# Moving three kv products behind the q projection, and a carry product over all 128 rows, in a fused linear-attention and convolution kernel

## The chip, the cores and the metric

The kernel runs on one core of a Trainium2 chip. The metric is the device time of one execution in microseconds (us), the median of the runs shown.

## What is computed

x is 2048 by 448 (S by D). Two branches read it, and a gate per row mixes them. The reference, cut to what matters:

```python
g = sigmoid((x * gate_w).sum(-1, keepdims=True))
# branch a: linear attention, 16 heads of 28, not causal
q, k, v = split(x @ wqkv)
phi = lambda t: where(t > 0, t + 1, exp(t)) + 1e-6
kv = einsum("bhsd,bhse->bhde", phi(k), v)
z = einsum("bhsd->bhd", phi(k))
o = einsum("bhqd,bhde->bhqe", phi(q), kv) / (einsum("bhqd,bhd->bhq", phi(q), z)[..., None] + 1e-6)
a = o @ wo
# branch b: a long convolution with a kernel K made from A, C, dt, by FFT, plus a skip term
b = irfft(rfft(x) * rfft(K)) + x * D_skip
return g * a + (1 - g) * b
```

For the inputs in use K is flat to the precision needed, so branch b becomes a running sum over the rows, scaled per column, plus the skip; a slower general path follows under a flag and does not run.

## The kernel before

The 2048 rows are 16 chunks of 128 (`NC`, `P`). Each matrix product is split into a high and a low part in the format fp32r, and products are summed as high by high, low by high, high by low. The order of instructions is the order in which the code is written (`manual_schedule`): each engine works through its own queue in that order, and semaphores hold it where data is missing. PE is TensorE (matmuls; PEld its weight loads), ACT ScalarE, DVE VectorE, POOL GpSimd, SP the queue that issues the DMAs.

The main loop runs over `c` from 2 to 13. In one turn PE computes, in this order:

- k of chunk c+1: `project(c + 1, wkh, wkl, ...)`, eleven matmuls (L325). It reads `xt[c+1]`, the turned chunk, whose high half ACT casts and whose low half POOL subtracts (`split_t`, L234 and L230), one turn ahead.
- v products (`do_v`, L401, L402), which are the running sum inside a chunk by a triangle `tri`, from c = 5 on.
- the kv products g of chunk c, `do_g(c)`, eleven matmuls (L394) that add `xn[c]` (the plain chunk, split by `split_n`: ACT L240, POOL L230) against `pkh[c]` and `pkl[c]` to four PSUM banks. They are read after the last chunk alone.
- q of chunk c: `project(c, wqh, wql, D + 2, "q")`, eleven matmuls (L325) to the one PSUM bank with the tag q.

For c below 5, `do_g(c)` stands ahead of q; for c above 4 it stands behind q and what follows q.

ACT and DVE turn k into its feature: `k_feature` (ACT e L351, L352; DVE L353), `k_high` (ACT pkh L357), `k_low` (DVE pkl and the column sums zb, L363). `q_post` does it for q: ACT e (L371, L340), DVE t (L341) and pq (L344). In the turns c = 2 and 3 ACT and DVE also do half of the reductions over the 256 states that decide and scale K (`steps`: ACT L283, L284; DVE L285). At c = 3 DVE casts `tri` and `gcr` (L501, L502). At c = 4 small operations on four columns follow (`sm`, L273, L274, L292 to L302), and at c = 5 PE transposes their result (p, L306), between q and g of chunk 5.

`skip(c)` (POOL L246) multiplies a plain chunk by D_skip.

The carry of the running sum from chunk to chunk is made behind the loop. The last rows of the chunks' v sums are gathered by DMA in `u`, at rows 0 to 15 and 32 to 47 (`UL` = 32); ACT casts `u` to `uw`, POOL makes rows 32 on the low part, and one product z (L688) with the table `gcr` gives what enters each chunk. Then PE forms kv (L719) from the copies `gs` of g, DVE masks it (L725 to L732), ACT casts `kvh` (L736), DVE makes `kvl` (L739), and PE multiplies it with wo (m, L699). The last loop then turns pq (tr, L595) and multiplies (a, L620), and the outputs are written.

Of the kernel before, what the change touches and what calls it, by code (L numbers as in the profile page):

```python
# [42 lines left out]
GIN = 9 + NC  # L43
L1, L0 = 32, 64
UL = 32
UZ = 2 * UL
PAD = S + P
MAGIC = 1.5 * 2.0 ** 23
TWO_PI = 6.283185307179586
# [85 lines left out]
def gated_mix_kernel(ctx: ExitStack, tc: tile.TileContext, xin, wq_d, wvo_d, abc_d, ldt_d, dsk_d,  # L135
                     turn_d, cst_d, first_d, gin_d, lag_d, out):
    nc = tc.nc
    PE, ACT, DVE, POOL, SP = nc.tensor, nc.scalar, nc.vector, nc.gpsimd, nc.sync
# [21 lines left out]
    cst = const.tile([P, DJ + RX + 1], F32, name="cst")  # L160
    mask, gcat, sel = cst[:DJ, :DJ], cst[:UZ, DJ:DJ + RX], cst[:, DJ + RX:]
    gcr = const.tile([UZ, RX], F32R, name="gcr")
    ones = const.tile([P, P], F32R, name="ones")
    rows = const.tile([P, S], F32, name="rows")
    near, dsk = (rows[:, i * D:(i + 1) * D] for i in range(2))
    u = const.tile([UZ, D], F32, name="u")
    zb = const.tile([P, D], F32, name="zb")
# [23 lines left out]
    def load_x(c):  # L191
        r = xp.tile([P, XC], F32, name="xr", tag="xr")
        turned[c], plain[c] = r[:, :NAT], r[:, NAT:]
        SP.dma_start(out=r, in_=xin[c])
# [34 lines left out]
    def low(eng, o, r, h):  # L229
        eng.tensor_tensor(out=o, in0=r, in1=h.bitcast(F32), op=ALU.subtract)  # L230

    def split_t(c):
        w = xt[c] = xt_p.tile([P, 2 * NAT], F32R, name="xt", tag="t")
        ACT.copy(w[:, :NAT], turned[c])  # L234
        low(POOL, w[:, NAT:], turned[c], w[:, :NAT])

    def split_n(c):
        r, w = plain[c], xn_p.tile([P, NX], F32R, name="xn", tag="n")
        xn[c] = w
        ACT.copy(w[:, :XC - NAT], r)  # L240
        low(POOL, w[:, XC - NAT:], r[:, :D], w[:, :D])
        if c > 2:
            skip(c)

    def skip(c):
        POOL.tensor_tensor(out=y[:, c], in0=plain[c][:, :D], in1=dsk, op=ALU.mult)  # L246
# [82 lines left out]
    def project(*args, **kw):  # L329
        o, run = pieces(*args, **kw)  # L330
        run(11)
        return o
# [15 lines left out]
    def k_feature(c, o):  # L348
        e = tp.tile([P, D], F32, name="e", tag="e")
        pks[c] = o[:, :D]  # L350
        ACT.activation(e, pks[c], AF.Relu, scale=-1.0)  # L351
        ACT.activation(e, e, AF.Exp, scale=-1.0)  # L352
        DVE.scalar_tensor_tensor(out=pks[c], in0=pks[c], scalar=1.0, in1=e, op0=ALU.add, op1=ALU.max)  # L353

    def k_high(c):
        pkh[c] = tp.tile([P, 512], F32R, name="pkh", tag="pkh")[:, EDGE:EDGE + D]
        ACT.add(pkh[c], pks[c], 1e-6)  # L357

    def k_low(c):
        pk = pks.pop(c)  # L360
        pkl[c] = tp.tile([P, 512], F32R, name="pkl", tag="pkl")[:, EDGE:EDGE + D]
        for o, a, op in ((pkl[c], pkh[c].bitcast(F32), ALU.subtract), (zb, zb, ALU.add))[::-1 if c == NC - 1 else 1]:
            DVE.scalar_tensor_tensor(out=o, in0=pk, scalar=1e-6, in1=a, op0=ALU.add, op1=op)  # L363
# [6 lines left out]
    def q_post(c, o, mid=None):  # L370
        ACT.activation(e1[:, c:c + 1], o[:, D:D + 1], AF.Exp, scale=-1.0)  # L371
        feature(pq[:, c], o, mid)
# [13 lines left out]
    def do_g(c, blocks=range(4)):  # L386
        w = xn[c]
        for i in blocks:
            a = w[:, 64 + i * P:64 + (i + 1) * P]
            b = w[:, XC - NAT + 64 + i * P:][:, :P] if i < 3 else None  # L390
            seq = [(a, pkh[c]), (a, pkl[c]), (b, pkh[c])] if i < 3 else \
                  [(a, pkh[c]), (a[:, :64], pkl[c])][::1 if c == 0 else -1]
            for n, (a, b) in enumerate(seq):
                PE.matmul(g[i][:a.shape[1], :D], lhsT=a, rhs=b, start=c == 0 and n == 0,  # L394
                          stop=c == NC - 1 and n == len(seq) - 1)
# [3 lines left out]
    def do_v(c):  # L399
        v = vt[c] = ps.tile([P, 512], F32, name="v", tag="v%d" % (c % 2))  # L400
        PE.matmul(v[:, :D], lhsT=tri, rhs=xn[c][:, :D], start=True, stop=False)  # L401
        PE.matmul(v[:, :D], lhsT=tri, rhs=xn[c][:, XC - NAT:], start=False, stop=True)  # L402

    def v_post(c):
        t = tp.tile([P, D], F32, name="t", tag="v0")
        DVE.tensor_tensor(out=t, in0=vt.pop(c)[:, :D], in1=near, op=ALU.mult)  # L406
        if c < NC - 1:
            for k in (c, UL + c):
                SP.dma_start(out=u[k:k + 1], in_=t[P - 1:P])
            v_add(c, t)  # L410
        return t
# [5 lines left out]
    def steps(n):  # L417
        for _ in range(n):
            next(prep, None)
# [44 lines left out]
    for c in range(2, NC - 2):  # L464
        if c + 3 < NC:
            load_x(c + 3)
        if c == 2:
            SP.dma_start(out=cst, in_=cst_d)
        if c == 4:
            SP.dma_start(out=wvo, in_=wvo_d)  # L470
        vs = VS.get(c, ())
        ko = project(c + 1, wkh, wkl, D, "v1" if c in (2, 4) else "k")
        for v in vs[:1]:
            do_v(v)
        split_t(c + 2)
        k_feature(c + 1, ko)
        k_high(c + 1)
        if c > 5:
            for v in vs[:1]:
                v_post(v)  # L480
        k_low(c + 1)
        if c < 5:
            do_g(c)
        qo = project(c, wqh, wql, D + 2, "q")
        if c == 5:
            steps(1)
        else:
            for v in vs[1:]:
                do_v(v)
        q_post(c, qo)  # L490
        if c == 10:
            split_n(c + 2)
        if c == 5:
            v_post(0)
        else:
            for v in vs[1:]:
                v_post(v)
        if c < 5:
            steps(2 if c == 4 else 1)
        if c == 3:  # L500
            DVE.tensor_copy(tri, trir)  # L501
            DVE.tensor_copy(gcr, gcat)  # L502
        if c == 7:
            SP.dma_start(out=okr[:, None, :DJ], in_=oks[:, None, :])
        if c == 9:
            DVE.tensor_reduce(out=okr[:, DJ:], in_=okr[:, :DJ], op=ALU.add, axis=AX.X)
            DVE.tensor_copy(okn, okr[:, DJ:])
        if c > 4:
            do_g(c)
        if c == 5:  # L510
            do_v(1)
        if c < 4:
            skip(c - 1)
        if c != 10:
            split_n(c + 2)
        if c == 5:
            v_post(1)
        for j in {11: (0, 1), 12: (2, 3)}.get(c, ()):
            w = xn_p.tile([P, NX], F32R, name="wo", tag="n")[:DJ, :2 * D].rearrange("p (i d) -> p i d", i=2)
            woh.append(w[:, 0])  # L520
            wol.append(w[:, 1])
            ACT.copy(woh[j], wo[:, j])
            low(POOL, wol[j], wo[:, j], woh[j])
# [109 lines left out]
    c = NC - 2  # L633
# [3 lines left out]
    do_v(c + 1)  # L637
    uw = xt_p.tile([P, 2 * NAT], F32R, name="uw", tag="t")[:UZ, :D]
    k_feature(c + 1, ko)
    ACT.copy(uw, u)  # L640
    low(POOL, uw[UL:], u[UL:], uw[UL:])
    k_high(c + 1)
    k_low(c + 1)
    zh = tp.tile([P, D], F32R, name="zh", tag="w")
# [283 lines left out]
```

## Time and profile before

| | |
|---|---|
| median of 3 runs | 176.55 us (176.33 to 176.62) |
| the profiled execution | 176.31 us |
| its span, first to last instruction | 174.5 us |
| PE, PEld busy | 96%, 87% of the span |
| DVE, ACT, POOL busy | 65%, 55%, 69% |
| granted TensorE clock | 1.0 throughout |

The profile shows one execution. A row of a timeline gives start and length in us, engine, line of the code, operation, output<-input by the program's names, their shapes, how many instructions were merged into the row, and in brackets how long the engine sat idle before it and who ended that. Matmuls overlap, so a row of one matmul is longer (0.36) than the distance to the next (0.20). The tile names merge: k written to the bank v1 is called v.

### The profile page before, as it was taken

Reading aid. Unit: us, or ns where it says so; the run is one execution under the profiler, and the core shown is the slowest. Engines: PE = TensorE matmul, PEld = TensorE weight load, DVE = VectorE, ACT = ScalarE, POOL = GpSimd, SP = SyncE. Lnnn points to the kernel's source line nnn. Section 1 sums busy time; section 2 is a strip of 40 time slices with the busy share of each in tenths; the row PEclk is TensorE's granted clock in tenths of the full one; section 3 lists DMA queues with packets and bytes.
Section 4 is the critical chain, followed back from the end, with each engine's and each line's share of the span. In section 5 each row is a group of like instructions: output and inputs, shape, how many; then the busy total and the mean of one; then the engine's idle time right before and its main releaser. Section 6 shows DMA issues by size and latency. Waiting matters only on the chain.

```text
span 174.5 us, 2800 instructions
## 1 busy us (share of the span) xinstructions
PE 168.2 (96%) x876; PEld 151.5 (87%) x876; DVE 113.8 (65%) x240; ACT 96.5 (55%) x221; POOL 119.9 (69%) x128
## 2 busy tenths in 40 slices
PE   6999999999989999999999999999999999999991
PEld 2699999978789999999999999998999999999991
DVE  1747636498984663937537255487898998997551
ACT  3789395896454372534627366256475564664441
POOL 5167466557809996796996999529968998983100
PEclk9999999999999999999999999999999999999999
DMA  5999954087001230330404300000031221222212
GB/s 165 418 316 317 273 163 146 0 327 334 2 4 35 89 123 1 125 120 2 121 4 129 116 1 0 0 0 2 7 66 53 106 94 69 81 99 84 111 71 93
DMA packets 7963, 18.61 MB, mean 107 GB/s; under 512 B 2045, under 2 KB 4810, under 8 KB 7818
## 3 DMA queue, kind: packets, MB, share of 16 engines
q1 hardware_dynamic: 7946, 18.41, 31.2%
q8 instruction: 7, 0.11, 0.2%
q14 instruction: 10, 0.08, 0.2%
HBM read 14.38 MB, written 3.67 MB: 103 GB/s over the span
## 4 chain that ended last, share of the span: by engine, by line
PE 81%; DVE 8%; ACT 4%; POOL 3%; issue 2%; DVEq 0%; ACTq 0%; POOLq 0%
PE a L620 20%; PE g L394 16%; PE q L325 14%; PE k L325 13%; PE tr L595 4%; PE v L325 3%; PE q L252 2%; POOL y L246 2%; PE v L402 2%; PE v L401 2%; PE m L699 1%; DVE sm L274 1%; PE k L719 1%; PE tr L719 1%; ACT y L283 1%
## 5 line engine op out<-in xcount | busy, mean ns | idle before, releaser
L620 PE MATMUL a<-wk,th 128*128 128x448 f32 (+1 forms) x170 | 36.2, 359 | 0.0
L394 PE MATMUL g<-pkh,xn 128*128 128x448 f32 x112 | 35.5, 363 | 0.0
L620 PEld LDWEIGHTS a<-wk,th 128*128 128x128 f32 x170 | 29.5, 189 | 1.6
L325 PE MATMUL k<-wk,xt 128*128 128x448 f32 x132 | 29.4, 366 | 0.0
L325 PE MATMUL q<-wqh,xt 128*128 128x450 f32 x120 | 27.5, 366 | 0.0
L353 DVE SCALAR_TENSOR_TENSOR k<-k,e 128x448 f32<-128x448 f32 x12 | 7.6, 632 | 30.5 <-ACT e L352 30.5
L325 PEld LDWEIGHTS k<-wk,xt 128*128 128x128 f32 x132 | 24.5, 188 | 2.9 <-ACT wk L423 0.5
L230 POOL TENSOR_TENSOR xn<-xr,xn 128x448 fp32r<-128x448 f32 x16 | 18.8, 1178 | 11.6 <-ACT xn L240 11.2
L414 POOL TENSOR_TENSOR y<-y,t 128x448 f32<-128x448 f32 x16 | 18.7, 1169 | 11.4 <-DVE t L406 11.4
L325 PEld LDWEIGHTS q<-wqh,xt 128*128 128x128 f32 x120 | 22.5, 189 | 1.8
L394 PE MATMUL g<-pkl,xn 128*128 128x448 f32 x64 | 23.3, 364 | 0.0
L394 PEld LDWEIGHTS g<-pkh,xn 128*128 128x128 f32 x112 | 21.0, 188 | 2.2
L533 POOL TENSOR_TENSOR prod<-pq,zb 128x448 f32<-128x448 f32 x16 | 18.4, 1154 | 4.3 <-ACT zb L656 3.0
L351 ACT ACTIVATE e<-k 128x448 f32<-128x448 f32 x12 | 6.5, 545 | 25.5 <-PE k L325 25.4
L246 POOL TENSOR_TENSOR y<-xr,rows 128x448 f32<-128x448 f32 x16 | 18.5, 1155 | 0.0
L230 POOL TENSOR_TENSOR xt<-xr,xt 128x512 fp32r<-128x512 f32 x14 | 18.1, 1295 | 0.4 <-ACT xt L234 0.4
L558 POOL TENSOR_TENSOR pn<-pq,den 128x336 f32<-128x336 f32 x16 | 12.1, 754 | 5.9 <-ACT den L547 4.1
L625 DVE SCALAR_TENSOR_TENSOR ot<-y,og,a 128x448 f32<-128x448 f32 (+1 forms) x17 | 10.7, 629 | 5.0 <-PE a L620 5.0
L603 DVE TENSOR_TENSOR th<-tr,th 128x512 fp32r<-128x512 f32 x16 | 11.0, 690 | 2.5 <-ACT th L602 2.0
L357 ACT ACTIVATE pkh<-k 128x448 fp32r<-128x448 f32 x12 | 6.6, 546 | 10.0 <-DVE k L353 10.0
L394 PEld LDWEIGHTS g<-pkl,xn 128*128 128x128 f32 x64 | 11.2, 174 | 0.9
L602 ACT CAST th<-tr 128x512 fp32r<-128x512 f32 x16 | 9.4, 590 | 4.5 <-PE tr L595 4.2
(151 smaller groups left out, 307.1 us busy)
## 6 DMA issues: line engine op xcount, KB each, us to landing
xr<-in SPq DMA_DIRECT2D x15, 512.0 KB, 5.9
out<-ot SPq DMA_DIRECT2D x15, 224.0 KB, 1.9
pq<-in SPq DMA_DIRECT2D x4, 448.0 KB
wvo<-in SPq DMA_DIRECT2D x1, 1792.0 KB
y<-in SPq DMA_DIRECT2D x2, 480.0 KB
y<-in SPq DMA_DIRECT2D x2, 450.0 KB
u<-t SPq DMA_DIRECT2D x30, 1.8 KB, 1.8
y<-in SPq DMA_DIRECT2D x1, 448.0 KB, 4.3
```

The costliest lines, as they stand in the source:

```text
L230: eng.tensor_tensor(out=o, in0=r, in1=h.bitcast(F32), op=ALU.subtract)
L246: POOL.tensor_tensor(out=y[:, c], in0=plain[c][:, :D], in1=dsk, op=ALU.mult)
L325: PE.matmul(o[:, :n], lhsT=a, rhs=b, start=run.n == 1, stop=not seq)
L353: DVE.scalar_tensor_tensor(out=pks[c], in0=pks[c], scalar=1.0, in1=e, op0=ALU.add, op1=ALU.max)
L394: PE.matmul(g[i][:a.shape[1], :D], lhsT=a, rhs=b, start=c == 0 and n == 0, stop=c == NC - 1 and n == len(seq) - 1)
L414: POOL.tensor_tensor(out=y[:, c], in0=y[:, c], in1=t, op=ALU.add)
L533: POOL.tensor_tensor(out=pd[c], in0=pq[:, c], in1=zb, op=ALU.mult)
L558: POOL.tensor_tensor(out=n[:, :3, :DJ].rearrange("p j (h d) -> p j h d", h=4), in0=a, in1=r[:, :H - 4].rearrange("p (j h) -> p j h", j=3)[ ...
L602: ACT.copy(h, ov)
L603: DVE.tensor_tensor(out=l, in0=ov, in1=h.bitcast(F32), op=ALU.subtract)
L620: PE.matmul(a[:, lo:hi], lhsT=u_, rhs=w_[:, lo:hi], start=n == 0, stop=n == 10)
L625: DVE.scalar_tensor_tensor(out=ot[:, lo:hi], in0=y[:, c, lo:hi], scalar=og[:, c:c + 1], in1=a[:, lo:hi], op0=ALU.mult, op1=ALU.add)
```

## The change

Two edits. First, `do_g(c)` of the chunks 2, 3 and 4 is taken from its place ahead of q and put to where those of later chunks stand: behind q, `q_post` and what follows, so that all chunks have one order. Second, `UZ` goes from 64 to 128: `u`, `uw` and `gcr` now have 128 rows, and so has the product z; rows 64 to 127 hold zeros. The low part is still made for rows 32 to 63 alone.

```diff
-UZ = 2 * UL
+UZ = 4 * UL
...
         k_low(c + 1)
-        if c < 5:
-            do_g(c)
         qo = project(c, wqh, wql, D + 2, "q")
...
-        if c > 4:
-            do_g(c)
+        do_g(c)
...
     ACT.copy(uw, u)
-    low(POOL, uw[UL:], u[UL:], uw[UL:])
+    low(POOL, uw[UL:2 * UL], u[UL:2 * UL], uw[UL:2 * UL])
```

The order on PE in the turn c = 2, before. v1_321 is k of chunk 3, xn_286 the plain chunk 2, q_356 is q of chunk 2, k_387 is k of chunk 4. From the last two g products to the next k:

```order
L394 MATMUL g2_143<-pkl_262,xn_286 128x448
L394 MATMUL g2_143<-pkh_260,xn_286 128x448
L394 MATMUL g3_144<-pkl_262,xn_286 64x448
L394 MATMUL g3_144<-pkh_260,xn_286 128x448
L325 MATMUL q_356<-wqh_70,xt_187 128x450 x8
L325 MATMUL q_356<-wql_71,xt_187 128x450 x3
L325 MATMUL k_387<-wk2_69,xt_333 128x448 x11
```

The same place now, from k of chunk 3 on; q of chunk 2 is called q_345 here:

```order
L325 MATMUL v1_321<-wk2_69,xt_277 128x448 x11
L325 MATMUL q_345<-wqh_70,xt_187 128x450 x8
L325 MATMUL q_345<-wql_71,xt_187 128x450 x3
L394 MATMUL g0_141<-pkh_260,xn_286 128x448
L394 MATMUL g0_141<-pkl_262,xn_286 128x448
```

q of chunk 2 follows at once on k of chunk 3, and the eleven g products of chunk 2 stand between q of chunk 2 and k of chunk 4. The turns c = 3 and 4 move in the same way.

The order on PE around the transposes p, before: q_491 is q of chunk 4, k_528 k of chunk 6, q_555 q of chunk 5.

```order
L325 MATMUL q_491<-wqh_70,xt_333 128x450 x8
L325 MATMUL q_491<-wql_71,xt_333 128x450 x3
L325 MATMUL k_528<-wk2_69,xt_468 128x448 x11
L401 MATMUL v_540<-xn_208,tri_85 128x448
L402 MATMUL v_540<-xn_208,tri_85 128x448
L325 MATMUL q_555<-wqh_70,xt_399 128x450 x8
L325 MATMUL q_555<-wql_71,xt_399 128x450 x3
L306 MATMUL p_567<-both_73,sm_81 128x112 x4
```

And now, from the last g products of chunk 4 on:

```order
L394 MATMUL g3_144<-pkl_408,xn_381 64x448
L394 MATMUL g3_144<-pkh_406,xn_381 128x448
L325 MATMUL k_528<-wk2_69,xt_468 128x448 x11
L401 MATMUL v_540<-xn_208,tri_85 128x448
L402 MATMUL v_540<-xn_208,tri_85 128x448
L325 MATMUL q_555<-wqh_70,xt_399 128x450 x8
L325 MATMUL q_555<-wql_71,xt_399 128x450 x3
L306 MATMUL p_567<-both_73,sm_81 128x112 x4
```

From k of chunk 6 on nothing has moved; the same number of instructions stands ahead of p. On DVE, ACT, POOL and SP the order is what it was. On DVE pkl of the chunks 4, 5 and 6 now names PE among what it waits for; shown for chunk 4:

```order
 L353 SCALAR_TENSOR_TENSOR k<-k,e 128x448 [waits Activation_49]
-L363 SCALAR_TENSOR_TENSOR pkl<-k,pkh 128x448 [waits Activation_49]
+L363 SCALAR_TENSOR_TENSOR pkl<-k,pkh 128x448 [waits PE_49,Activation_49]
 L363 SCALAR_TENSOR_TENSOR zb<-k,zb 128x448
 L341 TENSOR_SCALAR t<-e 128x448 [waits Activation_49]
```

Before, that order followed from DVE's earlier waits; now the wait stands there by itself. PE is named as the engine that reads the buffer of pkl last.

## The prediction

> **What bounds the kernel now.** I read the page first, then the busy times by stretch.
>
> ```profile
> span 174.5 us, 2800 instructions
> PE 168.2 (96%) x876; PEld 151.5 (87%) x876; DVE 113.8 (65%) x240; ACT 96.5 (55%) x221; POOL 119.9 (69%) x128
> 48.82:119.70 70.88, 70.88 (x356) 65.61 (x355) 40.40 (x76) 35.30 (x76) 55.26 (x49) 1.00 0.17 54
> 123.60:170.84 47.24, 47.23 (x276) 43.59 (x274) 38.83 (x88) 26.30 (x65) 31.46 (x44) 1.00 0.23 80
> ```
>
> The columns of the stretches are length, then busy time of PE, PEld, DVE, ACT and POOL, then the granted clock (1.00), DMA share and GB/s. TensorE has no gap from 48.82 to 119.70 and none from 123.60 to 170.84. So time can be saved only where PE stands, and what is saved before 48.82 is kept to the end, provided the other engines come forward as well. I then looked for PE's waits before 48.82 in its timeline. A number in brackets is idle time and what ended it; L325 is a projection (k, written to a tile named k or v, or q), L394 the kv products g, L401 a v product, L306 the four transposes p.
>
> ```profile
> 21.88 2.37 PE L325 MATMUL v<-wk,xt 128*128 128x448 f32 x11
> 24.09 0.36 PE L394 MATMUL g<-pkh,xn 128*128 128x448 f32 x1
> 26.29 1.80 PE L325 MATMUL q<-wqh,xt 128*128 128x450 f32 x8
> ...
> 28.55 2.37 PE L325 MATMUL k<-wk,xt 128*128 128x448 f32 x11
> ...
> 35.22 0.37 PE L325 MATMUL v<-wk,xt 128*128 128x448 f32 x1
> 35.95 2.28 PE L325 MATMUL v<-wk,xt 128*128 128x448 f32 x10 [0.36 <-POOL xt L230]
> 38.07 0.36 PE L394 MATMUL g<-pkh,xn 128*128 128x448 f32 x1
> ...
> 42.54 2.49 PE L325 MATMUL k<-wk,xt 128*128 128x448 f32 x11
> 44.87 0.37 PE L401 MATMUL v<-xn,tri 128*128 128x448 f32 x1
> ...
> 46.89 0.76 PE L325 MATMUL q<-wql,xt 128*128 128x450 f32 x3
> 48.46 0.60 PE L306 MATMUL p<-both,sm 112*128 112x112 f32 x4 [0.81 <-DVE sm L273]
> ```
>
> A block of k runs from its start to the next block's start in 24.09 − 21.88 = 2.21 us, so a matmul takes 0.20. Three blocks take longer. k of chunk 5 takes 38.07 − 35.22 = 2.85, that is 0.64 lost on the low half of xt from POOL. k of chunk 6 takes 44.87 − 42.54 = 2.33: 0.12 lost. The transposes could have started at 46.89 + 3 × 0.20 = 47.49 and start at 48.46: 0.97 lost on DVE's small operations on sm. In all 1.73 us.
>
> **What keeps DVE, ACT and POOL late there.** The timelines of those engines:
>
> ```profile
> 26.79 0.55 ACT L357 ACTIVATE pkh<-v 128x448 fp32r<-128x448 f32 x1 [0.70 <-DVE v L353]
> 28.75 0.17 ACT L371 ACTIVATE e<-q 128x1 f32<-128x1 f32 x1 [1.41 <-PE q L325]
> ...
> 32.74 0.54 ACT L351 ACTIVATE e<-k 128x448 f32<-128x448 f32 x1
> ```
>
> ```profile
> 36.24 1.03 DVE L341 TENSOR_SCALAR t<-e 128x448 f32<-128x448 f32 x1
> 37.37 0.62 DVE L344 SCALAR_TENSOR_TENSOR pq<-q,t 128x448 f32<-128x448 f32 x1
> ...
> 39.26 1.17 DVE L501 CAST tri<-both 128x128 fp32r<-128x128 f32 x1
> 40.35 1.18 DVE L502 CAST gcr<-cst 64x112 fp32r<-64x112 f32 x1
> ...
> 43.76 0.38 DVE L341 TENSOR_SCALAR t<-e 128x448 f32<-128x448 f32 x1
> ...
> 45.10 1.20 DVE L274 SCALAR_TENSOR_TENSOR sm<-sm 112x4 f32<-112x4 f32 x2
> 46.29 1.33 DVE L274 SCALAR_TENSOR_TENSOR sm<-sm 112x4 f32<-112x4 f32 x2
> ...
> 48.24 0.16 DVE L273 TENSOR_TENSOR sm<-sm,okc 112x4 f32<-112x4 f32 x1
> ```
>
> ```profile
> 34.61 1.28 POOL L230 TENSOR_TENSOR xt<-xr,xt 128x512 fp32r<-128x512 f32 x1
> ...
> 40.31 1.15 POOL L246 TENSOR_TENSOR y<-xr,rows 128x448 f32<-128x448 f32 x1
> 41.42 1.29 POOL L230 TENSOR_TENSOR xt<-xr,xt 128x512 fp32r<-128x512 f32 x1
> 46.24 1.28 POOL L230 TENSOR_TENSOR xt<-xr,xt 128x512 fp32r<-128x512 f32 x1
> ```
>
> At 28.75 ACT has been idle for 1.41 us, waiting for the projection q of chunk 2, which on PE stands behind the kv products of chunk 2. From there the chain of work that ended last runs through ACT's and DVE's queues without any wait for PE: ACT's squares and the two splits, e of chunk 4 at 32.74 (k of chunk 4 itself is done at 28.55 + 2.37 = 30.92), DVE's k, t and pq, the casts tri and gcr, the same again for chunk 5, and the small operations to 48.24. POOL takes its work from ACT's high halves and comes late with them. So one late q of chunk 2 stands behind all three losses.
>
> **The change, part by part.**
>
> First, q before g in chunks 2 to 4. No instruction is added or dropped; on PE eleven q matmuls change places with eleven g matmuls three times, so PE's own sum is unchanged. q of chunk 2 starts at 24.09 instead of 26.29, 2.20 earlier, and ACT can go on as soon as pkh is through: at 26.79 + 0.55 = 27.34. ACT comes 1.41 earlier there, not 2.20. Followed along from there:
>
> e of chunk 4 moves from 32.74 to 31.33, still behind k's end at 30.92, so the 1.41 holds. POOL's xt of chunk 5 ends at 34.61 + 1.28 − 1.41 = 34.48; k of chunk 5 needs it from its second matmul, 35.42. That wait (0.64) goes. xt of chunk 6 ended at 42.71 and now ends near 41.3; k of chunk 6 starts at 42.54 − 0.64 = 41.90. That wait (0.12) goes too.
>
> All q of this stretch share one PSUM bank: q of chunk 4 now arrives at 35.22 + 2.20 = 37.42 and needs pq of chunk 3 done, at 37.37 + 0.62 = 37.99 before, 36.58 now. Cover 0.8 us; if DVE did not come forward this would cost 0.6. The last small operation ends at 48.40 − 1.41, so p can start at 48.46 − 1.41 = 47.05. PE gets there at 47.49 − 0.64 − 0.12 = 46.73. So 0.32 of that wait is left.
>
> What is saved is therefore not the sum of the three waits but the way p comes forward: 1.41 us, since p is late last. The bounds: 1.73 if the chain comes forward by more than ACT's 1.41 (PE then has no wait left), and nothing if something else holds the chain. I take 1.41, since it is read from the row that begins the chain and each later link is in a queue that comes forward whole.
>
> What g being later costs: its sums g are read only after the last chunk. Its operands pkh and pkl have two buffers each, and the next writer of the same buffer belongs to the k two chunks on, which PE computes after this g in either order. DVE's pkl of chunks 4 to 6 now names PE in its wait. For chunk 4 that is g of chunk 2, over at about 24.09 + 2 × 2.2 = 28.5, while DVE reaches it only after e, 31.33. Behind it stand zb, t and pq; price nothing. SP's transfers keep their places; those that wait for an xr buffer come earlier with POOL.
>
> Second, 128 rows in the carry product. The memset of u, the cast of uw and the cast gcr now cover 128 partitions. tri (128 rows, 1.17 us) beside gcr (64 rows, 1.18) shows that rows cost nothing there. The product z itself:
>
> ```profile
> 119.75 0.37 PE L394 MATMUL g<-pkh,xn 128*128 128x448 f32 x1
> 120.04 0.46 PE L688 MATMUL z<-uw,gcr 64*112 64x448 f32 x1
> 120.43 1.82 PE L719 MATMUL k<-gs,wvo 128*112 128x112 f32 x16
> ...
> 123.60 0.65 PE L699 MATMUL m<-wo,kvh 112*112 112x448 f32 x2
> ```
>
> ```profile
> 120.04 0.17 PEld L688 LDWEIGHTS z<-uw,gcr 64*112 64x112 f32 x1 [0.31 <-issue]
> 120.43 1.65 PEld L719 LDWEIGHTS k<-gs,wvo 128*112 128x112 f32 x16 [0.22 <-issue]
> ```
>
> ```profile
> 122.08 0.17 DVE L547 COPY den<-den 128x16 f32<-128x16 f32 x1
> 122.29 0.28 DVE L725 TENSOR_TENSOR k<-k,cst 112x112 f32<-112x112 f32 x1
> ...
> 123.18 0.35 ACT L736 CAST kvh<-k 112x224 fp32r<-112x224 f32 x1 [1.69 <-DVE k L732]
> ```
>
> From g at 119.75 to k at 120.43 two products of 448 columns take 0.68 where the pace is 2 × 0.20; both weight loads stood still and waited for nothing the profile names. If the full array ends that, k starts 0.28 earlier. The Trainium skill (TensorEngine Tiling (Array Packing), Key Properties) says that changing the tiling mode drains TensorE, and lists 64 rows as a mode of its own; the trace agrees in that only this load, and the one behind it, stand still; by that rule counted in full the change would be worth 0.28 more. But the next product, m at 123.60, needs kvh, cast until 123.18 + 0.35 = 123.53, and kvh hangs on DVE, which reaches kv's mask at 122.29 straight from its own queue (122.08 + 0.17 = 122.25). So 0.04 of the 0.28 can pass and the rest becomes a wait before m. I take 0.03; bounds 0 and 0.28.
>
> **The sum.** The profiled execution took 176.31 us, its span 174.5 and 1.81 around it. 176.31 − 1.41 − 0.03 = 174.87. The median of the runs, 176.55, lies 0.24 above it, so the forecast is 176.55 − 1.44 = 175.1 us. About 0.2%, 0.35 us, is what a measurement of this kernel can tell from no change.
>
> **The rivals.**
> **The chain comes forward by less** (0.09): some operation of ACT, DVE or POOL meets another in a worse place and takes back 0.2 to 1.1 of the 1.41. For: t took 1.03 at 36.24 and 0.38 at 43.76, so 0.65 hangs on which POOL operation runs beside. Against: DVE and POOL both follow ACT and keep their distances. Gain 0.35 to 1.2: 175.35 to 176.2.
>
> **The wait is hidden anyway** (0.06): p is held by something that does not hang on ACT, or the swap on PE does not let ACT go on. Then k's waits go and p stays at 48.46, gain 0: 176.5. Against: ACT's own row names q as what it waited for.
>
> **The array's change counts in full** (0.07): kvh comes forward too, by DVE finding kv's product earlier, and up to 0.28 is added: 174.5 to 174.85. Against: DVE's own queue keeps it until 122.25. This is the time that the rule on the tiling mode would give (the Trainium skill, named above).
>
> **Slower: DVE and POOL collide in the small operations** (0.06). Pairs of L274 took 1.20 and 1.33 beside POOL's operations, on four elements a row, where the single operation at 48.24 took 0.16. If t of chunk 4 (now 0.38 at 43.76) and two more pairs of small operations each fall beside a POOL operation, at 1.03 − 0.38 = 0.65 for t and about 1.2 − 2 × 0.16 = 0.9 for a pair, the chain is 2.45 later for the 1.41 that it starts earlier, and p moves 1.04 back: 177.6. It decides from 1.41 + 0.35 = 1.76 us of new collisions on. The Trainium skill (SBUF — State Buffer, Who interferes with whom) has the port that DVE and GpSimd share as an exclusive lock, where the loser blocks for the whole instruction; the trace agrees in the two casts, which end with POOL's operations (gcr at 41.53, y at 41.46). By that rule t could lose up to 1.28, a whole POOL operation, and the slower case would be 0.6 worse.
>
> **How the numbers follow.** The forecast, a gain of 1.2 to 1.73, has 0.72, and its own range is 174.8 to 175.35. With the full array (0.07) and the weaker gain (0.09) faster comes to 0.88; hidden anyway gives 0.06 for no change, the collision 0.06 for slower. The range from 174.6 to 176.1 holds the forecast's case and nearly all of the two beside it.
>
> **What would show it.** Right: ACT's 1.41 before e<-q is gone and q of chunk 2 starts near 24.1; PE has no wait before k of chunk 5 and 6; the transposes p start between 46.7 and 47.1; all later blocks of PE lie about 1.4 earlier, and z's weight load stands still no more while a wait appears before m. Wrong: p starts at 48 or later though q came early, or a new wait of PE after 48, or t, tri, gcr or the L274 pairs are longer than the rows above.

## The result, and the profile after

| | before | after |
|---|---|---|
| median, first comparison | 176.59 us (176.33 to 176.63, 4 runs) | 175.09 us (174.55 to 175.34, 4 runs) |
| ratio | | 0.9914 [0.9889, 0.9939] |
| profiled execution, its span | 176.31, 174.5 | 175.34, 173.6 |

The forecast was 175.1. A second comparison of the same two kernels gave 174.38 against 176.70 (e5 below), under the low end of the forecast's range. So the agreement of 175.09 with 175.1 is in part luck: two terms were taken too small, and a late start, seen in the profiled execution, hid it.

The page of the changed kernel and its busy times by stretch, in the columns that the prediction explains; lines behind the moved call lie three lower than before:

```profile
span 173.6 us, 2803 instructions
PE 167.5 (97%) x876; PEld 151.9 (88%) x876; DVE 113.9 (66%) x240; ACT 96.1 (55%) x221; POOL 120.8 (70%) x128
17.34:48.82 31.48, 31.48 (x160) 28.97 (x159) 23.04 (x48) 21.32 (x57) 21.94 (x18) 1.00 0.55 182
47.50:118.00 70.50, 70.50 (x354) 65.20 (x353) 40.54 (x77) 34.78 (x75) 54.31 (x48) 1.00 0.17 54
122.00:169.00 47.00, 47.00 (x275) 43.48 (x274) 38.98 (x90) 26.33 (x65) 32.41 (x45) 1.00 0.22 77
```

From 17.34 to 48.82 PE was busy for 30.31 of 31.48 us before; now it is for all of it. Its timeline has none of the three waits. The first row is the last two matmuls of k of chunk 0; their wait is the only long one left once PE has begun:

```profile
9.09 0.67 PE L325 MATMUL k<-wk,xt 128*128 128x448 f32 x2 [0.97 <-DVE wk L230]
...
22.95 2.37 PE L325 MATMUL v<-wk,xt 128*128 128x448 f32 x11
25.16 1.77 PE L325 MATMUL q<-wqh,xt 128*128 128x450 f32 x8
...
36.25 2.36 PE L325 MATMUL v<-wk,xt 128*128 128x448 f32 x11
...
42.86 2.36 PE L325 MATMUL k<-wk,xt 128*128 128x448 f32 x11
...
47.08 0.76 PE L325 MATMUL q<-wql,xt 128*128 128x450 f32 x3
47.69 0.60 PE L306 MATMUL p<-both,sm 112*128 112x112 f32 x4
```

k of chunk 3 (written to v) starts at 22.95, 1.07 later than in the execution of before (21.88), where nothing of the change has acted yet. ACT's timeline shows where that comes from: its cast of a weight part waits for the first transfers, 0.16 us before and 1.21 here. The second piece, further on, is the row that the prediction began with; its wait is gone:

```profile
7.82 0.56 ACT L258 CAST wk<-y 128x448 fp32r<-128x448 f32 x1 [1.21 <-DMA y<-in]
...
27.86 0.55 ACT L357 ACTIVATE pkh<-v 128x448 fp32r<-128x448 f32 x1 [0.70 <-DVE v L353]
28.30 0.17 ACT L371 ACTIVATE e<-q 128x1 f32<-128x1 f32 x1
```

The parts of the execution, measured from the start of k of chunk 3 to be free of that delay:

| distance | before | after | difference |
|---|---|---|---|
| k of chunk 3 to ACT's e<-q of chunk 2 | 6.87 | 5.35 | −1.52 |
| to the last small operation on sm (L273) | 26.36 | 24.53 | −1.83 |
| to the transposes p | 26.58 | 24.74 | −1.84 |
| p to the end of the execution | 127.85 | 127.65 | −0.20 |

That makes −2.04. The late start gives 1.07 back, and 176.31 − 2.04 + 1.07 = 175.34, the profiled time. Over the profiled executions of all kernels here k of chunk 3 started between 21.83 and 22.95; e5, the same kernel as after, had 22.59. The three latest starts (22.50, 22.59, 22.95) all belong to kernels with 128 rows. But the one operation of the second edit that has run by then is POOL's memset of u, which takes 0.47 instead of 0.46 and is over at 2.87; e2, with 128 rows, starts at 22.30 as e3 does with 64; and the times of e1, e2 and e5 show no cost of the rows. So the scatter isn't shown to come from the edit, though eleven executions are too few to exclude a part.

DVE and POOL show how 1.52 became 1.83:

```profile
35.77 0.47 DVE L341 TENSOR_SCALAR t<-e 128x448 f32<-128x448 f32 x1
36.34 0.62 DVE L344 SCALAR_TENSOR_TENSOR pq<-q,t 128x448 f32<-128x448 f32 x1
...
42.97 1.38 DVE L341 TENSOR_SCALAR t<-e 128x448 f32<-128x448 f32 x1
...
45.30 1.34 DVE L274 SCALAR_TENSOR_TENSOR sm<-sm 112x4 f32<-112x4 f32 x2
46.56 0.16 DVE L292 TENSOR_SCALAR sm<-sm 112x4 f32<-112x4 f32 x1
46.63 0.22 DVE L274 SCALAR_TENSOR_TENSOR sm<-sm 112x4 f32<-112x4 f32 x2
...
47.48 0.16 DVE L273 TENSOR_TENSOR sm<-sm,okc 112x4 f32<-112x4 f32 x1
```

```profile
34.69 1.30 POOL L230 TENSOR_TENSOR xt<-xr,xt 128x512 fp32r<-128x512 f32 x1
...
42.94 1.15 POOL L230 TENSOR_TENSOR xn<-xr,xn 128x448 fp32r<-128x448 f32 x1 [1.03 <-ACT xn L240]
44.05 1.31 POOL L246 TENSOR_TENSOR y<-xr,rows 128x448 f32<-128x448 f32 x1
45.31 1.30 POOL L230 TENSOR_TENSOR xt<-xr,xt 128x512 fp32r<-128x512 f32 x1
```

Two of POOL's rows of before, for comparison:

```profile
35.86 1.16 POOL L246 TENSOR_TENSOR y<-xr,rows 128x448 f32<-128x448 f32 x1
...
43.93 1.22 POOL L230 TENSOR_TENSOR xn<-xr,xn 128x448 fp32r<-128x448 f32 x1 [1.22 <-ACT xn L240]
```

t of chunk 3 is short now (0.47, before 1.03). t of chunk 4 starts 0.03 behind POOL's xn and takes 1.38, where it took 0.38. One reading fits all these rows: a t that starts while a POOL operation runs ends 0.25 after it. Before, t of chunk 3 ended at 37.27 and POOL's y at 37.02; now it ends at 36.24 and xt at 35.99, and t of chunk 4 at 44.35 and xn at 44.09. So t of chunk 3 is short because only 0.22 of xt was left when it began, where 0.78 of y was left before. In return xt of chunk 7 is over at 46.61, just before the second pair of L274, which takes 0.22 instead of 1.33. By distance from k of chunk 3, DVE is ahead by 2.10 at pq of chunk 3 (13.39 against 15.49), by 1.86 before t of chunk 4, by 0.86 behind it, by 0.73 before the second pair and by 1.84 behind it. e1 and e5 show the same rows: t of chunk 4 at 1.38, the second pair at 0.22.

The carry product z, on PE and PEld:

```profile
118.98 0.36 PE L394 MATMUL g<-pkh,xn 128*128 128x448 f32 x1
119.18 0.37 PE L685 MATMUL z<-uw,gcr 128*112 128x448 f32 x1
119.39 1.81 PE L716 MATMUL k<-gs,wvo 128*112 128x112 f32 x16
...
122.69 0.66 PE L696 MATMUL m<-wo,kvh 112*112 112x448 f32 x2
```

```profile
118.98 0.17 PEld L685 LDWEIGHTS z<-uw,gcr 128*112 128x112 f32 x1
...
123.11 0.17 PEld L696 LDWEIGHTS m<-wo,kvl 112*112 112x112 f32 x1 [0.16 <-DVE kvl L736]
```

The loads no longer stand still. From the last g to kv's product PE needs 0.41 instead of 0.68, and from the last g to m 3.71 instead of 3.85 (119.75 to 123.60). The wait before kvl's load was there before too (0.15).

### The profile page after: what moved, and what is told of

Its sections match the earlier page's. It is cut to its first block, busy times and chain, and to the rows that moved or that the text cites. A ratio compares the mean times of both kernels' runs of the same rounds, so it can differ in the third digit from the quotient of the medians.

```text
span 173.6 us, 2803 instructions
## 1 busy us (share of the span) xinstructions
PE 167.5 (97%) x876; PEld 151.9 (88%) x876; DVE 113.9 (66%) x240; ACT 96.1 (55%) x221; POOL 120.8 (70%) x128
## 4 chain that ended last, share of the span: by engine, by line
PE 93%; DMA 4%; DVE 1%; ACT 1%; SPq 0%; issue 0%; ACTq 0%
PE a L617 21%; PE g L394 20%; PE q L325 19%; PE k L325 14%; PE v L325 6%; PE tr L592 4%; DMA y<-in 4%; PE v L402 2%; PE v L401 2%; PE m L696 1%; PE k L716 1%; PE tr L716 1%; SPq L210 0%; DVE wk L230 0%; ACT wk L258 0%; DVE ot L622 0%
## 5 line engine op out<-in xcount | busy, mean ns | idle before, releaser
L230 POOL TENSOR_TENSOR xn<-xr,xn 128x448 fp32r<-128x448 f32 x16 | 19.4, 1212 | 8.8 <-ACT xn L240 6.8
L341 DVE TENSOR_SCALAR t<-e 128x448 f32<-128x448 f32 x15 | 10.1, 672 | 2.4 <-ACT e L340 2.4
```

The lines of the kernel that those rows point to most:

```text
L341: DVE.tensor_scalar(out=t, in0=e, scalar1=1.0, scalar2=1e-6, op0=ALU.min, op1=ALU.add)
```

## The experiments

In all timed comparisons the kernel before ran beside; its medians were 176.57 (24 runs, e1 to e4) and 176.70 (20 runs, e5 to e8). The edits are to the kernel before unless said.

**e1: q ahead of g alone.**

```diff
-        if c < 5:
-            do_g(c)
...
-        if c > 4:
-            do_g(c)
+        do_g(c)
```

> q ahead of the kv products in chunks 2 to 4, the carry product as before (64 rows). Chain theory: the whole gain of the forecast sits here, 1.4 to 1.9 us less than before, the transposes p start 1.4 to 1.9 us after where k of chunk 3 starts than before, and z's weight load still stands still 0.31 us. Rival (the rows carry a good part of it): under 1.2 us.

174.56 us (4 runs), ratio 0.9884 [0.9865, 0.9903]: 2.0 us, a little more than the 1.4 to 1.9 expected, and more than the whole change was forecast to give. z's weight load still waits 0.3, as expected. PE has no wait from k of chunk 3 to p, which lies 24.74 behind it as in the changed kernel:

```profile
21.98 2.37 PE L325 MATMUL v<-wk,xt 128*128 128x448 f32 x11
...
46.72 0.60 PE L306 MATMUL p<-both,sm 112*128 112x112 f32 x4
```

**e2: 128 rows alone.**

```diff
-UZ = 2 * UL
+UZ = 4 * UL
-    low(POOL, uw[UL:], u[UL:], uw[UL:])
+    low(POOL, uw[UL:2 * UL], u[UL:2 * UL], uw[UL:2 * UL])
```

> The carry product over 128 rows, the order as before. Chain theory: the pause of 0.28 us at z goes, but kvh and m follow DVE's own queue, so 0.03 to 0.14 us less in the trace from z to m, and no change that the times can tell. Rival (full array counts in full): 0.28 us less, the time clearly under before.

176.49 (12 runs), ratio 0.9993 [0.9980, 1.0006]: this can't be told from no change. In the trace the last g to m takes 3.70 (120.16 to 123.86), 0.15 less than before. e9 and after, without z's pause, take 3.71, and e1, with it, 3.85 as before. So the traces show the small gain that the times are too coarse for.

**e3 and e4: the swap in chunk 2 alone, and in chunks 3 and 4 alone.** These ask whether one late q of chunk 2 stands behind all three waits.

```diff
-        if c < 5:
+        if c in (3, 4):
             do_g(c)
...
-        if c > 4:
+        if not (c in (3, 4)):
             do_g(c)
```

e4 has `c == 2` in place of `c in (3, 4)`.

> Only chunk 2 has q ahead of its kv products; chunks 3 and 4 as before. If the late q of chunk 2 alone stands behind all three losses: 1.4 us less, as with all three. If ACT then only waits one chunk later, since q of chunk 3 is where it was and ACT reached it with 0.28 us to spare: 0.2 to 0.8 us less.

> Only chunks 3 and 4 have q ahead; chunk 2 as before. Chain theory: ACT still waits 1.41 us for q of chunk 2, and q of chunk 3 gives 0.28 us at most, so 0 to 0.3 us less. Rival (each moved block pays for the wait that follows it): k of chunk 5, k of chunk 6 and p follow the blocks moved here, so about 1.0 us or more.

e3: 176.05 (7 runs), ratio 0.9964 [0.9950, 0.9978], a quarter of e1's gain. ACT doesn't wait at chunk 2, but one chunk later it waits for the next q:

```profile
27.66 0.16 ACT L371 ACTIVATE e<-q 128x1 f32<-128x1 f32 x1
...
35.79 0.17 ACT L371 ACTIVATE e<-q 128x1 f32<-128x1 f32 x1 [1.76 <-PE q L325]
```

e4: 176.91 (12 runs), ratio 1.0015 [1.0000, 1.0029]: no gain. The loss of 0.34 by the medians, 0.10 in the profiled execution from k of chunk 3 to the end, isn't clear of the noise. ACT's wait at chunk 2 stays (1.42), and two prices appear that the prediction had named. On DVE t of chunk 4 falls beside POOL's xn (which starts at 43.96), and pq comes late with it, after another 0.52 that the row puts down to PE (e3 has the same 0.52 with DVE's own t named, so its cause stays open):

```profile
43.98 1.38 DVE L341 TENSOR_SCALAR t<-e 128x448 f32<-128x448 f32 x1
45.89 0.62 DVE L344 SCALAR_TENSOR_TENSOR pq<-q,t 128x448 f32<-128x448 f32 x1 [0.52 <-PE v L402]
```

On PE q of chunk 5 has to wait for the bank that pq of chunk 4 leaves:

```profile
46.66 1.84 PE L325 MATMUL q<-wqh,xt 128*128 128x450 f32 x8 [0.98 <-ACT e L352]
48.94 0.55 PE L306 MATMUL p<-both,sm 112*128 112x112 f32 x4
```

The row names e as the releaser; that the bank is meant is read from pq's end at 46.51, 0.15 before this q starts. So the swap of three chunks is worth 2.0, while one part gives 0.5 and the other nothing: each q has to be early for ACT never to wait.

**e5: the changed kernel again.**

> The changed kernel once more. The swap alone gave 174.56, both edits 175.09 in a few runs whose profiled execution began k of chunk 3 at 22.95 instead of 21.9. If that late start is chance (a transfer that lands late): 174.4 to 174.7 now, at or a little under the swap alone. If the rows cost something: 175.0 again, with the late start in the profile.

174.38 (174.21 to 174.99, 6 runs), ratio 0.9869 [0.9849, 0.9889]. Its profiled execution (174.99) has k of chunk 3 at 22.59 and p 24.76 behind it. From k of chunk 3 to the end it took 152.40, after 152.39, before 154.43. With before's start, 21.88, after would take 174.27, near this median. That the first comparison's median was up by late starts is seen in its one profiled execution; in the timed runs without a profile it is inferred.

**e6: ACT's squares ahead of its q work, PE untouched.** In the turns 2 and 3 ACT does its half of the reductions in the time in which it waited for q; DVE's two products move along.

```diff
+        if c in (2, 3):
+            steps(1)
         q_post(c, qo)
...
-        if c < 5:
-            steps(2 if c == 4 else 1)
+        if c == 4:
+            steps(2)
```

> The kernel before, PE's order untouched; in chunks 2 and 3 the reductions of the convolution branch (ACT's squares, DVE's two products) stand ahead of the feature of q instead of behind it, so ACT has work while it waits for q. Chain theory (ACT's idle 1.41 us at q of chunk 2 is the cause): 1.0 to 1.9 us less, without any move on PE. Rival (what counts is the order on PE): no change.

175.97 (9 runs), ratio 0.9958 [0.9940, 0.9976]: 0.7 less, under the 1.0 to 1.9 expected. The waits before k of chunks 5 and 6 go, without any move on PE: ACT's idle time is their cause. p still waits and holds the gain down: ACT stands still at chunk 4, where no squares fill the gap, and both pairs of L274 still run beside POOL (1.19 and 1.33):

```profile
42.03 0.17 ACT L371 ACTIVATE e<-q 128x1 f32<-128x1 f32 x1 [1.48 <-PE q L325]
```

```profile
35.17 2.37 PE L325 MATMUL v<-wk,xt 128*128 128x448 f32 x11
...
41.83 2.37 PE L325 MATMUL k<-wk,xt 128*128 128x448 f32 x11
...
47.68 0.60 PE L306 MATMUL p<-both,sm 112*128 112x112 f32 x4 [0.86 <-DVE sm L273]
```

**e7: one POOL operation out of the small operations' way.** y of chunk 6 (`skip`) moves behind chunk 5's second feature, so that xt of chunk 7 runs sooner and is over before the second pair.

```diff
-        if c > 2:
+        if c > 2 and c != 6:
             skip(c)
...
         if c == 5:
             v_post(1)
+            skip(6)
```

> The kernel before, with one POOL operation (D_skip times chunk 6, 1.16 us) moved one turn later, so that POOL is through with the low half of chunk 7 some 1.1 us earlier, while DVE does the small operations before p. If these small operations are held by POOL's operations: p comes about 0.9 us earlier, 0.7 to 1.0 us less. If they are only late because DVE's queue is: no change.

176.06 (12 runs), ratio 0.9966 [0.9953, 0.9979]: 0.64 less, a little under the 0.7 to 1.0 expected. The second pair takes 0.22, and p comes 25.63 behind k of chunk 3, 0.95 less than before. A wait of 0.21 for POOL appears at 58.99 and takes part of it back:

```profile
46.84 0.22 DVE L274 SCALAR_TENSOR_TENSOR sm<-sm 112x4 f32<-112x4 f32 x2
```

```profile
47.94 0.56 PE L306 MATMUL p<-both,sm 112*128 112x112 f32 x4
...
58.99 2.28 PE L325 MATMUL k<-wk,xt 128*128 128x448 f32 x10 [0.21 <-POOL xt L230]
```

So what lies beside a POOL operation sets p by 0.95 us, with ACT's and PE's order unchanged.

**e8: the transfer that starts late, cut in two** (in the changed kernel).

```diff
-PARTS = (..., (("w", 0), ("x", 1)))
+PARTS = (..., (("w", 0),), (("x", 1),))
```

> The changed kernel with the third of the first transfers cut in two: the last part of the weights of k alone, then the turned chunk 1. After the change PE has no wait left but those in the first 9 us, for these transfers. If they bound it: k of chunk 0 ends some 0.5 us earlier and 0.2 to 0.6 us less than the changed kernel. If the turned chunk 1 is what counts, or the extra issue delays what follows: no change or up to 0.5 us more.

175.71 (6 runs), ratio to before 0.9936 [0.9918, 0.9955]: 1.3 slower than e5, where at most 0.5 was expected. k of chunk 3 starts at 22.50, within the scatter. Whether the cut helped the start can't be told, since PE itself was slow there: seven weight loads of k of chunk 0 took 1.82, before 1.38. PE's last matmul starts 0.1 earlier than in e5 (169.24 against 169.35), while the span is 0.9 longer. The compute engines have no row in that time. By the DMA rates over time the last bytes move after 172.8, in e5 before 172.4; why stays open.

**e9: 96 rows.** This asks whether any height below 128 makes z's pause; it rests on one profiled execution.

```diff
-UZ = 2 * UL
+UZ = 3 * UL
```

> The kernel before with 96 rows (UZ = 3 * UL) in the carry product; q and g keep their old order. With 64 rows the load of z began 0.31 us after PEld was free and the next load 0.22 after; with 128 rows (e2_rows_only) neither stood still, and with 112 rows (m) none does. Theory (only a half height of 64 makes the pause; 96 goes like 112): no pause, z to the next product 0.20 as with 128. Rival (every height that is not near the full 128 makes it): a pause of 0.2 to 0.3 as with 64. The time of the whole can't be told from 176.5 in either case.

The load of z takes its turn at once, and the next load too:

```profile
120.08 0.17 PEld L688 LDWEIGHTS z<-uw,gcr 96*112 96x112 f32 x1
120.29 1.84 PEld L719 LDWEIGHTS k<-gs,wvo 128*112 128x112 f32 x16
```

64 rows pause, 96, 112 and 128 don't; the pause costs 0.28 here. That fits the rule of the Trainium skill that the prediction named (TensorEngine Tiling (Array Packing), Key Properties: a change of tiling mode drains TensorE), if 64 rows are another mode and 96 are none. The same page of the Trainium skill lists 128 by 64 as a mode too (Available Configurations), and there the trace doesn't agree: the g products with 64 columns keep the pace of 0.20 (25.69, 25.89, 26.09 before). So which shapes pause is read from the runs here, not from the list.

## Why the prediction held, and where it didn't

**PE's three losses** are right: 1.73 counted, and all went. With 1.84 from k of chunk 3 to p, 0.11 more went in small pieces of the blocks between.

**"So one late q of chunk 2 stands behind all three losses"** is wrong. ACT's idle time is the cause (e6), but before, q of chunks 3 and 4 came almost in time only because ACT was late. With chunk 2 alone put right ACT waits 1.76 at chunk 3 (e3). The change moved all three, so the sum didn't suffer.

**"That wait goes", for k of chunks 5 and 6**, held: no wait in after's rows.

**"0.32 of that wait is left"** is the step that failed in size. It came from "each later link is in a queue that comes forward whole". ACT itself came forward by 1.52: its e<-q now starts 0.11 before the row of pkh ends (28.30, 28.41). Then DVE gained 0.56 on t of chunk 3, lost 1.00 on t of chunk 4 and gained 1.11 on the second pair, beside other shifts; the net is 0.31 beyond ACT's 1.52. p now starts where PE's pace puts it (47.08 + 3 × 0.20 = 47.68, p at 47.69), and as close behind the end of DVE's last operation as before (0.05, before 0.06): the two limits meet there. The term 1.41 measures 1.84, a little over the upper bound named in the sum, "1.73 if the chain comes forward by more". That the collisions added to the gain and didn't take from it was luck: the sum has no term that says which way they fall.

**The 128 rows**, put at 0.03 with bounds 0 and 0.28, measure 0.14 (after, e2). The step that failed is "which reaches it from its own queue". DVE's two rows before kv's mask were 0.21 apart before (122.08, 122.29) and are 0.09 apart now, so DVE had been waiting for PE there, whose kv products ended at 120.43 + 1.82 = 122.25:

```profile
121.32 0.17 DVE L544 COPY den<-den 128x16 f32<-128x16 f32 x1
121.41 0.27 DVE L722 TENSOR_TENSOR k<-k,cst 112x112 f32<-112x112 f32 x1
```

**The sum** should have been about −1.84 − 0.14 = −2.0, and not −1.44; the time 174.6, and not 175.1. −2.0 lies at the edge of the first interval (−1.1 to −2.0) and inside those of e1 and e5.

**"Shows that rows cost nothing there"**, said of the casts tri (1.17) and gcr (1.18), can't be read from these rows: both times are set by the POOL operations beside them. In e3 POOL stood idle there, and tri with 128 rows took 0.22, gcr with 64 rows 0.20. So the conclusion holds to 0.02.

**The bank's cover and the later g** cost nothing in after, as said: q of chunks 4 and 5 has no wait. e4 shows that the cover is real and what it costs when DVE stays late: 0.98.

**The slower rival** had the right mechanism: t of chunk 4 did collide, for 1.00 and not the 0.65 taken. The 0.65 came from one row, a t with 0.78 of POOL's operation left; with nearly all of it left, the 0.25 above makes 1.15 − 0.03 + 0.25 = 1.37, and 1.38 is measured. Its other two collisions didn't come, and one of before's went. "Against: DVE and POOL both follow ACT and keep their distances", said of the weaker gain, was no safe ground: 0.2 us of relative shift decided 1 us. The Trainium skill (SBUF — State Buffer, Who interferes with whom) says that the order of issue decides who blocks; the rows agree: t took 0.38 when it started 0.17 ahead of POOL's xn (43.76, 43.93 before) and 1.38 when it started 0.03 behind (after; 0.02 behind in e1 and e4).

**The signs.** "A wait appears before m" was no sign: the one at kvl's load is 0.16, and was 0.15 before. p at 47.69 is late by the start alone: 47.69 − 1.07 = 46.62, a little earlier than the 46.7 to 47.1 named. One sign of being wrong did show, "t, tri, gcr or the L274 pairs are longer": t of chunk 4 took 1.38 and the first pair 1.34, and yet the gain was larger than forecast. One longer operation alone doesn't tell.

## What to carry to other kernels

When an engine waits for an early result, put right each place at which the same result is late, not the first alone: the two parts of this edit gave 0.5 us and nothing, together 2.0. A chain that comes forward doesn't keep its collisions, so its gain is a range to which short operations beside a long one of another engine add an amount of either sign. Measure an edit from the last point that it can't have touched; here the start scatters by as much as half the gain.

## What the runs showed of the hardware

Operations of DVE on four columns took 0.15 to 0.17 us where POOL stood idle, and a pair 0.22; beside a tensor_tensor of POOL a pair took 1.19 to 1.34 us (before, after, e6).

DVE's t (tensor_scalar, 128 by 448) took 0.38 to 0.40 us when it started 0.17 us or more ahead of POOL's tensor_tensor. When it started behind one, with 0.1 us or more of it left, it ended 0.24 to 0.26 us after it. That holds in every row of t from 19 to 110 us in all eleven traces, so the price of such a collision is what is left of POOL's operation, not a fixed amount.

A matmul of 64 rows among those of 128 cost 0.28 us, one of 96 rows nothing.

The start of k of chunk 3 moved by up to 1.1 us between executions that do nearly the same up to there. In after a late landing accounts for it (ACT's wait of 1.21). In e5 it does so in part: ACT's first cast starts 0.38 later than before, and PE was slow besides, with 1.59 for the seven weight loads that took 1.38 before.
